# Linear attention and a squared-ReLU feed-forward: keys as weights, split denominators, a new sign step and a new order

## The chip, the cores and the metric

The kernel runs on one core of one Trainium2 chip. The metric is device time in microseconds (us). Three runs of the kernel before gave 237.81, 237.87 and 238.11 us; the median is 237.87 us. One further execution was recorded by the hardware profiler; it took 240.32 us.

## The reference

Four batches, four heads, 1088 positions, head size 32. Each position's q and k become 64 features: eight projections by S1 times eight by S2. For a batch and head, kv is the sum over positions of features times v, and z is the sum of the features; the output at a position is (q features · kv) / (q features · z + 1e-6). The heads side by side make x with 4352 rows and 128 columns, which passes through a feed-forward layer.

```python
def phi(x):
    a = np.einsum('rd,bhsd->bhsr', S1, x)
    b = np.einsum('rd,bhsd->bhsr', S2, x)
    return np.einsum('bhsi,bhsj->bhsij', a, b).reshape(*x.shape[:-1], r * r)
...
kv = np.einsum('bhsf,bhsd->bhfd', k_p, v)
z = np.sum(k_p, axis=2)
num = np.einsum('bhsf,bhfd->bhsd', q_p, kv)
den = np.einsum('bhsf,bhf->bhs', q_p, z)[..., None] + 1e-06
...
r = np.maximum(x @ w_in, 0.0)            # w_in 128 x 2048
return (s * (r * r) + b) @ w_out         # w_out 2048 x 128
```

S1, S2, w_in and w_out come to the chip as 64-bit floats, in two 32-bit words each; q, k and v are 32-bit.

## The kernel before

**Tiles and stages.** The 4352 rows are cut into tile 0 with 256 rows and tiles 1 to 8 with 512. For each batch b, `kvphase(b)` (L239) makes the key features and the matrix st[b] of kv and z: projections on TensorE, transposes on VectorE (L258, L263), the outer product of the two projections (L267), sums over positions on TensorE (L280), a masked copy of z (L294), and products that turn and spread the results (L302, L306). In the first batch keys and values come in three groups of three chunks of 128 positions, in the others in one. In the projections S is the weight and the keys are the moving operand, in quarters of the array. For each tile t, `direct_features` (tiles 0 and 1, L330 to L339) or `stored_features` (the others, with a way through DRAM, L350 to L369) make the q features, and `attend(t)` (L391 to L428) the numerators, denominators, reciprocals and x. Then eight steps `ffn(t, jp)` per tile (L471) do two blocks of 128 of the 2048 columns each: six products into hp, relu, square, and six products into the tile's output sum. In tile 0 the products are plain f32, two and two per step. In tiles 1 to 8 each operand is split into a high part of reduced f32 and a low rest, with three products for one (wih, wil, woh, wol, uh, ul, xh, xl). `finish(t)` (L512) scales the sum and stores it.

**Weights.** `to_float` (L197) makes an f32 of the two words of a 64-bit float in four instructions: the high word scaled (L113, on ScalarE or VectorE), the low word scaled (L119), a join (L190) and the sign put back (L186), the last two on VectorE. `split_weights` follows with the high part (a cast) and the low rest (L448). It is done for S, and for four blocks of 512 columns of w_in and four of w_out, named w0 to w7, even for w_in and odd for w_out.

**What sets the order.** Nothing is scheduled by the compiler. Each piece of work is a generator that issues an instruction group and yields. `ORDER`, a list of names written out, says which generator goes on next, and each engine takes its instructions in that order: y and z are products on constants that do no work for the result, Lx a DMA, s the phase of S, kb the key phase of batch b, qt and nt features and attend of tile t, wx a weight block, and two digits tj the step jp = j of tile t. `ON_DVE` lists the movable instructions that go to VectorE; the others go to ScalarE. All DMAs are issued by SP, in order. At the start they are: a third of the first values (192 KB), S (80 KB), q of tile 0 (128 KB), the first keys (three times 192 KB), q of tile 1 (256 KB), constants (96 KB), the other two thirds of the values, then weight blocks of 512 KB with q of tiles 2 and 3 (256 KB each) between them. The tiles run in the order 0, 1, 2, 3, 4, 5, 8, 6, 7. hp has two buffers of two PSUM banks, the small products share three banks, the output sum has one.

Of the kernel before, what the change touches and what calls it, by code (L numbers as in the profile page):

```python
# [27 lines left out]
NT = len(TILES)  # L28
NCH = 9
SP = NCH * P  # L30
KGROUPS = {0: (3, 3, 3), 1: (9,), 2: (9,), 3: (9,)}
EPS = 1e-6
DIRECT = (0, 1)
DEN_APART = (0,)
FIRST_F32 = (0, 1, 2, 3, 4, 5, 6, 7)
ORDER = """
y y y y y y y y y y y y y y y y y y y y z z z z z z z Lv0 Ls Lq0 Lk0 Lk0 Lk0 s s s Lq1 s Lcst s s s q0 Lv0 q0
Lv0 q0 k0 Lw0 q0 q0 q0 Lw2 k0 Lq2 k0 z k0 Lw1 k0 k0 k0 Lq3 q1 q1 k0 k0 k0 q1 k0 q1 q1 q1 w0 z k0 w0 k0 Lw3 k0
w2 w0 z k0 w2 Lw4 w0 q2 k0 w2 w0 n0 n0 w2 Lw5 q2 Lw6 w1 q3 q2 n0 w1 n0 n0 w2 n0 n0 q3 n0 w3 w2 q3 z 00 w3 w1
n1 00 w1 Lw7 00 w3 01 Lk1 w1 w0 w5 00 n1 01 n1 w5 02 01 n1 w4 w3 w4 q2 01 02 q2 w3 w4 q2 03 02 Lv1 w4 w6 02 q3  # L40
w6 Lq4 w4 04 03 q3 w6 q3 03 w5 05 04 w5 03 04 w6 w5 04 w1 05 n1 06 w7 05 w7 w6 w7 05 06 w7 07 06 n1 w7 06 n1
07 w7 k1 07 n1 w3 n1 07 k1 n1 11 k1 07 07 k1 07 10 11 k1 13 Lq8 10 11 10 12 11 10 11 q4 k1 10 12 10 q4 q2 12
q4 k1 12 13 11 k1 12 13 12 Lv2 w5 13 q3 k1 q8 w6 Lq5 k1 w4 n2 q8 13 15 q8 q4 q4 n2 n2 q4 14 n2 n2 n2 13 14 n2
n2 15 14 n3 15 Lv3 14 16 q8 14 n2 q8 14 q8 15 16 n2 17 16 15 16 22 17 n3 n3 17 n3 20 n3 16 17 15 n3 20 17 16
20 22 17 22 20 20 21 17 n3 22 17 n3 20 n3 21 22 24 21 q4 23 24 21 21 24 Lk3 21 n3 23 22 24 23 24 25 23 q8 27
25 23 23 25 27 27 25 24 27 26 25 25 27 26 Lk2 k2 26 26 32 26 31 32 26 k2 32 k2 k2 32 27 31 k2 30 27 31 27 k2
32 31 k3 31 30 33 30 k2 k3 k3 k2 35 30 33 30 Lq6 30 k3 35 31 35 33 32 k3 33 k2 35 k3 35 k2 q6 k3 q5 33 k3 34
q6 q6 q5 q5 k3 34 n4 k3 34 36 q6 n4 q6 34 n4 q6 37 n4 n4 36 34 33 36 37 36 34 n4 37 n4 n4 35 n4 n4 41 37 36 36
37 41 40 q6 41 37 41 40 41 43 37 40 37 42 43 40 40 43 44 42 43 n8 43 42 45 n8 q5 44 n8 q5 n8 40 n8 q5 44 n8 n8
41 n8 n8 n8 44 Lq7 46 42 42 42 44 45 43 45 46 47 45 q5 46 q7 45 n5 q7 47 44 q7 n5 47 n5 n5 45 n5 46 n5 n5 47  # L50
n5 n6 46 n5 46 n5 q7 q7 47 q7 50 n6 n6 47 n6 50 n6 n6 50 n6 51 n6 50 47 52 51 47 50 51 50 51 52 53 51 52 51 53
q7 52 53 n7 54 52 n7 56 n7 54 53 53 55 54 56 52 n7 54 n7 n7 53 56 n7 n7 54 57 56 55 54 56 81 55 57 57 80 55 55
55 57 81 57 56 81 80 57 81 82 57 81 57 84 80 82 82 80 83 80 82 80 82 83 81 83 84 82 83 84 83 85 84 86 85 84 85
87 86 85 n6 83 n6 n7 85 60 n7 87 84 86 87 86 85 87 86 61 87 60 86 60 61 62 61 60 60 61 64 61 62 87 62 64 65 87
62 87 87 64 87 60 62 64 61 64 65 63 65 66 63 65 65 63 70 66 62 66 63 67 63 63 67 64 67 66 65 66 67 66 70 67 67
70 71 67 70 67 72 71 70 70 71 72 73 72 71 71 74 72 73 72 71 74 73 76 74 73 75 73 74 72 76 74 76 77 75 75 76 73
76 75 74 77 75 75 77 76 77 77 77 77 77
"""
ON_DVE = frozenset("""
a7 a8 k0 q11 q25 q27 q31 q33 q34 q40 q53 q54 q55 q60 q64 q66 q67 q70 q73 q76 q80 q86 r15 r22 r32 r34 r37 r46  # L60
r64 r72 r80 r84 r86 sb t2 t3 u11 u12 u14 u15 u16 u20 u21 u24 u26 u27 u30 u35 u37 u40 u41 u42 u43 u50 u51 u53
u55 u56 u57 u60 u62 u65 u71 u73 u76 u77 u80 u81 u84 u86 w3h w4h w4m w5b w7b w7m x3 x4 x6 x8
# [27 lines left out]
def attn_ffn_kernel(ctx: ExitStack, tc: tile.TileContext, qT, kT, vp, s80, cst, w_in, w_out, outT):  # L90
# [22 lines left out]
    def scaled(key, out, in_, scale):  # L113
        if key in ON_DVE:
            nc.vector.tensor_scalar(out=out, in0=in_, scalar1=scale, scalar2=None, op0=ALU.mult)
        else:
            nc.scalar.activation(out=out, in_=in_, func=AF.Copy, scale=scale)

# [41 lines left out]
    def load_v(b):  # L160
        vt = p2.tile([P, NCH * H * D], F32, name="vt")
        vt = v_in[b] = vt.rearrange("p (c h d) -> p c h d", c=NCH, h=H)
        c = 0
        for n in KGROUPS[b]:
            nc.sync.dma_start(out=vt[:, c:c + n].rearrange("p c h d -> p (c h d)"),
                              in_=block(vp, (b * NCH + c) * H * D, n * H * D))
            c += n
            yield
# [8 lines left out]
    def load_weights(i, k):  # L177
        raw = p4.tile([P, 2 * CW], I32, name=f"raw{k}")
        nc.sync.dma_start(out=raw, in_=block((w_in, w_out)[k], i * CW, CW).bitcast(I32))
        w_raw[i, k] = raw  # L180
        yield
# [3 lines left out]
    def with_sign(out, high, t):  # L185
        nc.vector.scalar_tensor_tensor(out=out, in0=high, scalar=-0x80000000, in1=t,  # L186
                                       op0=ALU.bitwise_and, op1=ALU.bitwise_or)
# [9 lines left out]
    def to_float(key, out, raw, bits):  # L197
        low, high = words(raw)
        scaled(key + "m", out, f32(high), 2.0 ** -112)
# [4 lines left out]
        yield  # L204
        with_sign(out.bitcast(I32), high, out.bitcast(I32))
# [15 lines left out]
    def s_phase():  # L221
# [3 lines left out]
        nc.vector.tensor_copy(out=srep[:, 1].rearrange("p (i x) -> p i x", i=R),  # L225
                              in_=own[:, 1].unsqueeze(1).broadcast_to([P, R, R]))
# [387 lines left out]
```

## Time and profile before

| what | before |
|---|---|
| median of three runs without a profile | 237.87 us |
| profiled execution | 240.32 us |
| span from its first to its last instruction | 237.5 us |
| TensorE products busy | 228.6 us (96%) |
| TensorE weight loads | 176.0 us (74%) |
| VectorE busy | 207.5 us (87%) |
| ScalarE busy | 165.6 us (70%) |
| GpSimd busy | 2.9 us (1%) |
| mean granted clock of TensorE | 0.993 |
| DMA | 22.09 MB, mean 93 GB/s |

Busy times are shares of one profiled execution. TensorE's is the time in which at least one product is under way; products overlap, so a busy TensorE need not be at its peak. A row of the timeline gives the start of an instruction, its duration, the engine, the line, what it writes and reads, and in brackets how long the engine had been idle and what ended that. The chain of waits follows the work that ended last back to the start; each piece is a start, a duration and what ran. A granted clock of 1.00 is 2.4 GHz, one of 0.50 is 1.2 GHz.

### The profile page before, as it was taken

Reading aid. Unit: us, or ns where it says so; the run is one execution under the profiler, and the core shown is the slowest. Engines: PE = TensorE matmul, PEld = TensorE weight load, DVE = VectorE, ACT = ScalarE, POOL = GpSimd, SP = SyncE. Lnnn points to the kernel's source line nnn. Section 1 sums busy time; section 2 is a strip of 40 time slices with the busy share of each in tenths; the row PEclk is TensorE's granted clock in tenths of the full one; section 3 lists DMA queues with packets and bytes.
Section 4 is the critical chain, followed back from the end, with each engine's and each line's share of the span. In section 5 each row is a group of like instructions: output and inputs, shape, how many; then the busy total and the mean of one; then the engine's idle time right before and its main releaser. Section 6 shows DMA issues by size and latency. Waiting matters only on the chain.

```text
span 237.5 us, 4567 instructions
## 1 busy us (share of the span) xinstructions
PE 228.6 (96%) x1864; PEld 176.0 (74%) x1867; DVE 207.5 (87%) x275; ACT 165.6 (70%) x193; POOL 2.9 (1%) x13
## 2 busy tenths in 40 slices
PE   8688999999999999999999999999999999999993
PEld 3556877877887777778878678787878877888782
DVE  1879999999999989989999898999989998577972
ACT  2389978918899548717476677765697797668881
POOL 0000100000000000000000000000000000000000
PEclk9979999999999999999999999999999999999999
DMA  6999974549561002015115344000100001001001
GB/s 168 325 417 366 210 171 151 162 118 188 151 202 68 0 3 91 0 47 135 46 44 150 75 121 122 3 0 1 42 4 0 0 1 44 3 0 44 0 0 44
DMA packets 8948, 22.09 MB, mean 93 GB/s; under 512 B 992, under 2 KB 3424, under 8 KB 8928
## 3 DMA queue, kind: packets, MB, share of 16 engines
q1 hardware_dynamic: 8928, 21.81, 31.5%
q8 instruction: 14, 0.23, 0.4%
q14 instruction: 6, 0.05, 0.1%
HBM read 18.66 MB, written 3.15 MB: 92 GB/s over the span
## 4 chain that ended last, share of the span: by engine, by line
PE 82%; DVE 6%; DMA 4%; ACT 3%; issue 2%; SPq 1%; DVEq 0%; ACTq 0%
PE ops L469 35%; PE hp L469 35%; DMA qt<-qT 4%; PE psa L391 4%; PE psa L280 2%; DVE ul L463 2%; PE psa L350 2%; PE psa L253 1%; PE psa L306 1%; DVE u L133 1%; DVE ph L267 1%; ACT u L129 1%; ACT ot L523 1%; DVE pq L339 1%; DVE uh L111 1%
## 5 line engine op out<-in xcount | busy, mean ns | idle before, releaser
L463 DVE TENSOR_TENSOR ul<-u,uh 128x1024 fp32r<-128x1024 f32 x64 | 77.9, 1222 | 6.6 <-ACT uh L111 3.8
L129 ACT ACTIVATE u<-hp 128x1024 f32<-128x1024 f32 (+1 forms) x61 | 59.2, 970 | 34.2 <-DVE ul L463 18.8
L135 ACT ACTIVATE u<-u 128x1024 f32<-128x1024 f32 (+1 forms) x53 | 52.7, 996 | 5.8 <-DVE u L127 4.4
L469 PE MATMUL hp<-xh,wil 128*128 128x512 f32 x128 | 51.6, 403 | 0.0
L469 PE MATMUL ops<-uh,wol 128*128 128x512 f32 x128 | 50.3, 393 | 0.1
L469 PE MATMUL hp<-xh,wih 128*128 128x512 f32 x128 | 50.0, 390 | 0.0
L469 PE MATMUL hp<-xl,wih 128*128 128x512 f32 x128 | 49.9, 390 | 0.0
L469 PE MATMUL ops<-uh,woh 128*128 128x512 f32 x128 | 49.9, 390 | 0.0
L469 PE MATMUL ops<-ul,woh 128*128 128x512 f32 x128 | 39.8, 392 | 0.0
L111 ACT CAST uh<-u 128x1024 fp32r<-128x1024 f32 x30 | 31.4, 1050 | 8.2 <-DVE u L133 5.5
L469 PEld LDWEIGHTS hp<-xh,wil 128*128 128x128 f32 x128 | 24.0, 188 | 10.1 <-ACT u L129 2.9
L469 PEld LDWEIGHTS ops<-uh,wol 128*128 128x128 f32 x128 | 24.0, 188 | 6.1 <-ACT ot L523 0.5
L469 PEld LDWEIGHTS ops<-ul,woh 128*128 128x128 f32 x128 | 23.6, 188 | 6.0 <-DVE ul L463 1.2
L111 DVE CAST uh<-u 128x1024 fp32r<-128x1024 f32 x34 | 23.4, 690 | 5.2 <-ACT u L135 4.3
L469 PEld LDWEIGHTS hp<-xl,wih 128*128 128x128 f32 x128 | 24.0, 188 | 5.2
L469 PEld LDWEIGHTS ops<-uh,woh 128*128 128x128 f32 x128 | 24.0, 188 | 5.0
L469 PEld LDWEIGHTS hp<-xh,wih 128*128 128x128 f32 x128 | 24.0, 188 | 4.4
L133 DVE TENSOR_TENSOR u<-u 128x1024 f32<-128x1024 f32 x19 | 23.2, 1221 | 2.4 <-ACT u L129 2.3
L127 DVE TENSOR_SCALAR u<-hp 128x1024 f32<-128x1024 f32 x11 | 13.5, 1223 | 1.7 <-PE hp L469 0.9
L523 ACT ACTIVATE ot<-ops,bias,cst_sb 128x512 f32<-128x512 f32 (+1 forms) x10 | 7.0, 709 | 6.4 <-PE ops L469 6.4
L267 DVE TENSOR_TENSOR ph<-kab 128x768 f32<-128x768 f32 (+2 forms) x9 | 10.8, 1222 | 0.2
L391 PE MATMUL psa<-pq,st 64*32 64x256 f32 (+3 forms) x320 | 10.0, 350 | 0.0
(72 smaller groups left out, 172.9 us busy)
## 6 DMA issues: line engine op xcount, KB each, us to landing
pq<-qd SPq DMA_DIRECT2D x7, 512.0 KB
br<-qd SPq DMA_DIRECT2D x14, 256.0 KB
qt<-qT SPq DMA_DIRECT2D x8, 256.0 KB
raw<-w_in SPq DMA_DIRECT2D x4, 512.0 KB
raw<-w_out SPq DMA_DIRECT2D x4, 512.0 KB
outT<-ot SPq DMA_DIRECT2D x7, 256.0 KB
kt<-kT SPq DMA_DIRECT2D x3, 576.0 KB
vt<-vp SPq DMA_DIRECT2D x3, 576.0 KB
```

What stands on the lines that cost most here:

```text
L111: (nc.vector.tensor_copy if key in ON_DVE else nc.scalar.copy)(out=out, in_=in_)
L127: nc.vector.tensor_scalar(out=out, in0=in_, scalar1=0.0, scalar2=None, op0=ALU.max)
L129: nc.scalar.activation(out=out, in_=in_, func=AF.Relu)
L133: nc.vector.tensor_tensor(out=out, in0=in_, in1=in_, op=ALU.mult)
L135: nc.scalar.activation(out=out, in_=in_, func=AF.Square)
L267: nc.vector.tensor_tensor(out=ph[:, c0:c0 + m].rearrange("p c h i x -> p (c h) i x"), in0=a.unsqueeze(3).broadcast_to([P, H * m, R, R]), i ...
L280: nc.tensor.matmul(out[32 * q:32 * q + 32], w, x, start=(q not in begun), stop=last, skip_group_check=True)
L350: nc.tensor.matmul(ab[a:a + 32, :M], sq[:, 32 * w:32 * w + 32], qT_t[t][:, r * M:(r + 1) * M], start=True, stop=True, skip_group_check=True)
L391: nc.tensor.matmul(out[32 * h:32 * h + 32, e0:e1], st_t[b][64 * r:64 * r + 64, h // 2, h % 2, y], pq[64 * r:64 * r + 64, h, e0:e1], start= ...
L463: nc.vector.tensor_tensor(out=ul[:, :, :N], in0=u[:, :, :N], in1=f32(uh[:, :, :N]), op=ALU.subtract)
L469: nc.tensor.matmul(out, w, x, start=(first and k == 0), stop=(last and k == len(terms) - 1))
L523: nc.scalar.activation(out=ot[:, s], in_=o[:, s], func=AF.Identity, scale=s_col, bias=bias)
```

## The change

The change has these parts.

- In the first batch's key phase the keys become the weights and S (64 columns) the moving operand: one product of the full array per chunk of 128 positions. Its result has the positions on the partitions, so the transposes become copies (`first_keys`, k0). The host lays out the first batch's values to match.
- The first batch's sum of keys runs on a path of its own (`first_key_sums`, e0), the values' sums on another (`first_value_sums`, v0), and tile 0's denominators are made from the first alone (`first_denominators`, d0) before its numerators (`first_numerators`, n0).
- `to_float` loses the sign step: the high word goes through a Prelu on ScalarE whose slope for negative numbers is 2^32, and the join's shift leaves a sign from the exponent.
- The first 512 columns of each weight come in two blocks of 256, so there are ten weight blocks, w0 to w9, instead of eight.
- The last tile in the order (7) is finished in two halves, one on ScalarE with a DMA issued by ScalarE, one on VectorE with a DMA issued by SP. Tile 8 is finished in one.
- More constant products at the start, narrower ones (c, 256 columns) between the first phases.
- A new `ORDER` and a new `ON_DVE`; the tiles run 0, 1, 2, 3, 6, 4, 5, 8, 7.

```diff
+VGROUPS = {0: (3, 3, 3), 1: (9,), 2: (9,), 3: (9,)}
+WBLOCKS = (256, 256, 512, 512, 512)
...
+y y y y y y y y y y y y y y y y y y y y y y y y y y y y y y y y y y y y y y y z z z z z z Ls Lk0 Lk0 Lk0 s s
+Lv0 s Lv0 s s s Lv0 Lq0 k0 Lcst Lw0 k0 Lw1 k0 k0 e0 k0 Lw2 c e0 k0 k0 Lq1 v0 Lq2 k0 v0 k0 Lw3 e0 Lw5 c q0 q0
+e0 Lw4 v0 q0 e0 q0 q0 Lw6 w0 v0 q0 w0 Lq4 e0 w0 w1 c c v0 Lk1 w2 v0 w0 w2 w0 Lw7 c d0 q1 w2 w1 d0 w2 q2 w1 d0
+w3 q1 Lw9 d0 q1 d0 w3 Lw8 q1 q2 Lq8 q1 w3 c c n0 w5 q1 n1 w5 Lq5 n0 w4 w5 w4 00 q2 w5 w6 w5 01 w6 w4 00 q4 w6
+00 02 01 w6 q4 n1 Lq3 01 n1 00 q4 n1 n1 w4 Lv1 n1 03 02 w4 Lk3 01 w7 02 w7 04 n1 03 n1 n1 02 w9 03 w9 05 n1 04
+w9 03 04 q2 w7 w9 q2 10 w7 05 q2 w7 q4 05 w9 k1 q4 w3 q4 w8 w3 w8 04 k1 w1 k1 w8 05 10 k1 06 w8 13 10 06 06 07
+w1 10 k1 06 10 k1 w8 07 k3 k1 07 k1 13 k1 k3 07 13 w2 q2 11 13 w6 k1 12 07 11 07 07 13 10 11 k3 11 15 k3 12 n2
+11 12 11 n2 12 k3 15 16 12 12 15 16 n2 16 13 n2 n2 n2 15 14 n2 n2 16 n2 17 15 Lk2 n2 14 q3 Lv3 16 k3 Lv2 q3 14
+q3 17 k2 k3 14 20 k2 k2 17 14 21 q3 k3 q3 k2 20 q3 14 20 k2 15 q4 20 22 20 16 17 k3 17 17 k3 22 q3 q8 17 k2 22
+q8 17 21 q8 n3 k2 22 k2 23 Lq6 21 n3 n3 n3 24 n3 n3 n3 20 n3 n3 n3 21 q5 22 q6 k2 24 21 21 24 q6 23 q6 22 24
+23 q5 24 25 k2 23 n4 25 23 26 25 n4 q6 n4 q6 25 n4 q8 n4 23 n4 q8 26 q8 n4 n4 q6 24 25 26 27 26 26 n4 30 27 n4
+25 30 27 33 27 30 32 27 30 26 30 32 q5 32 27 33 33 32 31 27 32 34 27 33 31 30 33 31 q6 35 34 31 34 n6 31 Lq7
...
+74 73 76 74 73 74 75 76 74 72 74 76 77 75 76 73 76 75 75 77 74 75 77 75 77 76 77 77 77 77 77 77
+a5 a6 b00 k1 k2 q02 q03 q10 q14 q15 q22 q32 q33 q37 q41 q46 q47 q50 q52 q54 q66 q67 q81 r11 r13 r23 r45 r46
+r53 r56 r57 r65 r66 r70 r71 r72 r75 r84 r85 r87 s0 t3 u17 u23 u27 u31 u33 u37 u41 u44 u51 u53 u54 u57 u61 u63
+u67 u70 u72 u73 u74 u75 u77 u80 u81 u85 u86 w0h w5h w6h w7h x1 x2 x3 x6 x8 y0
...
-    def with_sign(out, high, t):
-        nc.vector.scalar_tensor_tensor(out=out, in0=high, scalar=-0x80000000, in1=t,
-                                       op0=ALU.bitwise_and, op1=ALU.bitwise_or)
...
     def to_float(key, out, raw, bits):
         low, high = words(raw)
-        scaled(key + "m", out, f32(high), 2.0 ** -112)
+        nc.scalar.activation(out=out, in_=f32(high), func=AF.Prelu, scale=2.0 ** -112, alpha=2.0 ** 32)
         yield
         scaled_up(key + "b", bits, low.bitcast(U32), 0.875 * 2.0 ** -29, 0.4999)
         yield
         join(out.bitcast(I32), out.bitcast(I32), bits)
-        yield
-        with_sign(out.bitcast(I32), high, out.bitcast(I32))
         yield
...
+        copy("s1", srep[:, 1].rearrange("p (i x) -> p i x", i=R), own[:, 1].unsqueeze(1).broadcast_to([P, R, R]))
+        yield
+        copy("s0", srep[:, 0].rearrange("p (i x) -> p i x", i=R), own[:, 0].unsqueeze(2).broadcast_to([P, R, R]))
...
+    def value_sums(add, out, b, ph, c):
+        for h in range(H):
+            add(h, out, v_in[b][:, c, h], ph[:, c, h].rearrange("p i x -> p (i x)"), c == NCH - 1)
+
+    def masked(out, zz):
+        nc.vector.tensor_tensor(out=out, in0=zz.rearrange("p (h x) -> p h x", h=H).unsqueeze(2).broadcast_to([P, H, R, R]),
+                                in1=mask.unsqueeze(3).broadcast_to([P, H, R, R]), op=ALU.mult)
+
+    def turn_values(out, kvs):
+        nc.tensor.matmul(out, kvs.rearrange("p r f -> p (r f)"), identity, start=True, stop=True, skip_group_check=True)
+
+    def spread(out, zm, first):
+        for h in range(H):
+            for r in range(2):
+                nc.tensor.matmul(out[64 * r:64 * r + 64, h], zm[:, h].rearrange("p i x -> p (i x)"), one32,
+                                 start=(first and h == 0), stop=True, skip_group_check=True)
+
+
+
+    first = {}
+
+    def first_keys():
+        kt = k_in[0]
+        kab = first["kab"] = p1.tile([P, 2, NCH, 32], F32, name="kab0")
+        ph = first["ph"] = p1.tile([P, NCH, H, R, R], F32, name="ph")
+        c0 = 0
+        for n in KGROUPS[0]:
+            ps = ps_a.tile([P, 512], F32, name="psa")[:, :64 * n]
+            for c in range(n):
+                a = (c0 + c) * P
+                nc.tensor.matmul(ps[:, 64 * c:64 * c + 64], kt[:, a:a + P], sk[:, :64],
+                                 start=(c == 0), stop=(c == n - 1), skip_group_check=True)
+            yield
+            copy(f"y{c0}", kab[:, :, c0:c0 + n], ps.rearrange("p (c w x) -> p w c x", w=2, x=32))
+            yield
+            outer(ph[:, c0:c0 + n], kab[:, 0, c0:c0 + n], kab[:, 1, c0:c0 + n], n)
+            yield
+            c0 += n
+
+    def first_key_sums():
+        zt = ps_a.tile([P, 512], F32, name="psa")
+        add = sums()
+        c0 = 0
+        for n in KGROUPS[0]:
+            for c in range(c0, c0 + n):
+                add(c % 4, zt[:, :32], first["kab"][:, 0, c], first["kab"][:, 1, c], c >= NCH - 4)
+            c0 += n
+            yield
+        zm = p2.tile([P, H, R, R], F32, name="zm")
+        masked(zm, zt[:, :32])
+        yield
+        parts = zt[:, P:2 * P].rearrange("p (h d) -> p h d", h=H)
+        spread(parts, zm, True)
+        yield
+        st = st_t[0] = const.tile([P, 2, 2, 2, 32], F32, name="st0")
+        copy("t0z", st[:, :, :, 1], parts.rearrange("p (j g) d -> p j g d", j=2))
+        yield
+
+    def first_value_sums():
+        kvp = ps_a.tile([P, 512], F32, name="psa")
+        add = sums()
+        c0 = 0
+        for n in KGROUPS[0]:
+            for c in range(c0, c0 + n):
+                value_sums(add, kvp[:, :64], 0, first["ph"], c)
+            c0 += n
+            yield
+        kvs = p2.tile([P, 2, 64], F32, name="kvs")
+        copy("k0", kvs, kvp[:, :64].unsqueeze(1).broadcast_to([P, 2, 64]))
+        yield
+        turned = ps_a.tile([P, 512], F32, name="psa")
+        turn_values(turned[:, :P], kvs)
+        yield
+        copy("t0v", st_t[0][:, :, :, 0], turned[:, :P].rearrange("p (j g d) -> p j g d", j=2, g=2))
+        yield
...
+    def first_denominators():
+        M = TILES[0] // 2
+        den = ps_h.tile([P, 2, 512], F32, name="hp")
+        parts_of(0, [den[:, r, :M] for r in range(2)], 1, qfeat[0], True)
+        yield
+        dt = p1.tile([P, NMAX], F32, name="dt")
+        nc.vector.transpose(out=dt[:, :2 * M].rearrange("p (r m) -> p r m", r=2), in_=den[:, :, :M])
+        yield
+        yield from inverse(dt[:, :2 * M], M // 32, first)
+
+    def first_numerators():
+        M = TILES[0] // 2
+        num = ps_h.tile([P, 2, 512], F32, name="hp")
+        parts_of(0, [num[:, r, :M] for r in range(2)], 0, qfeat[0], True)
+        yield
+        x = p2.tile([P, NMAX], F32, name="x")[:, :2 * M]
+        nc.vector.tensor_tensor(out=x.rearrange("p (r m) -> p r m", r=2), in0=num[:, :, :M],
+                                in1=first["rr"][:, :2 * M].rearrange("p (r m) -> p r m", r=2), op=ALU.mult)
+        x_first.append(x)
+        yield
...
+        if t == LAST:
+
+            M = N // 2
+            nc.scalar.activation(out=ot[:, :M], in_=o[:, :M], func=AF.Identity, scale=s_col, bias=bias)
+            yield
+            nc.vector.tensor_scalar(out=ot[:, M:N], in0=o[:, M:N], scalar1=s_col, scalar2=bias,
+                                    op0=ALU.mult, op1=ALU.add)
+            yield
+            nc.scalar.dma_start(out=block(outT, n0, M), in_=ot[:, :M])
+            yield
+            nc.sync.dma_start(out=block(outT, n0 + M, M), in_=ot[:, M:N])
+            yield
+            return
...
+    def keep_warm(n):
...
+        parts = (4, NCH, 32) if b else (1, NCH, P)
+        vp[:, b] = vpad[b].reshape(*parts, H, D).transpose(0, 2, 1, 3, 4).reshape(P, NCH, H, D)
```

Every other call of `copy`, `relu`, `squared` and `split_u` stays; where it runs follows from the new `ON_DVE`. The second, third and fourth batch keep the quarter-array projections and the transposes.

## Rows read from the trace of the kernel before

**Rows 1.** Stretches: start:end, length, busy us by engine, clock, DMA share, GB/s

```profile
10.00:20.00 10.00, 6.92 (x133) 4.41 (x142) 8.52 (x19) 7.25 (x15) 0.00 (x0) 0.83 1.01 390
20.00:30.00 10.00, 10.00 (x74) 8.11 (x59) 9.62 (x21) 9.81 (x18) 1.45 (x4) 1.00 1.02 269
```

**Rows 2.** Chain of waits in order of time: start us, us, what

```profile
18.76 1.13 PE hp L469 x4
...
32.48 0.87 PE ops L469 x4
33.35 1.11 PE psa L253 x16
...
233.62 0.78 ACT ot L523
```

**Rows 3.** Timeline to 13 us, instructions that waited for a DMA or follow one

```profile
3.47 0.27 ACT L117 ACTIVATE sk<-s_raw 128x80 f32<-128x80 f32 x1 [1.46 <-DMA s_raw<-s]
...
8.16 1.15 PE L330 MATMUL hp<-qt,srep 32*64 32x256 f32 x32 [0.24 <-DMA qt<-qT]
...
11.63 0.69 ACT L117 ACTIVATE w<-raw 128x512 f32<-128x512 f32 x1 [1.25 <-DMA raw<-w_in]
...
12.91 0.68 ACT L117 ACTIVATE w<-raw 128x512 f32<-128x512 f32 x1
```

**Rows 4.** Chain of waits, other pieces of TensorE

```profile
15.01 1.01 PE psa L350 x8
...
48.03 0.57 PE psa L350 x8
...
49.83 2.96 PE hp L469 x12
52.79 1.36 PE ops L469 x6
...
54.15 1.02 PE psa L391 x32
...
92.38 0.97 PE psa L253 x16
```

**Rows 5.** Groups of instructions by shape: count, busy us, mean ns, idle before

```profile
L186 DVE SCALAR_TENSOR_TENSOR w<-raw,w 128x512 int32<-128x512 int32 x8 | 5.4, 691 | 0.2
...
L267 DVE TENSOR_TENSOR ph<-kab 128x768 f32<-128x768 f32 x3 | 2.9, 958 | 0.1
...
L523 ACT ACTIVATE ot<-ops,bias,cst_sb 128x256 f32<-128x256 f32 x3 | 1.6, 555 | 0.0
...
L117 ACT ACT_TABLE_LOAD x1 | 1.3, 1283 | 0.7 <-PEq L604 0.7
...
L339 DVE TENSOR_TENSOR pq<-hp,br 128x512 f32<-128x512 f32 x2 | 1.3, 682 | 0.0
```

**Rows 6.** Timeline of ScalarE, consecutive instructions in two places

```profile
17.50 0.61 ACT L111 CAST wih<-w 128x512 fp32r<-128x512 f32 x1
18.01 0.37 ACT L111 COPY abq<-psa 128x256 f32<-128x256 f32 x1
18.27 0.68 ACT L117 ACTIVATE w<-raw 128x512 f32<-128x512 f32 x1
18.84 0.68 ACT L123 ACTIVATE raw<-raw 128x512 int32<-128x512 uint32 x1
...
27.37 0.60 ACT L129 ACTIVATE u<-hp 128x512 f32<-128x512 f32 x1
28.00 0.63 ACT L135 ACTIVATE u<-u 128x512 f32<-128x512 f32 x1
28.54 0.60 ACT L111 CAST woh<-w 128x512 fp32r<-128x512 f32 x1
```

**Rows 7.** Stretches of 1 us, TensorE: busy us, clock, DMA share, GB/s

```profile
11.00:12.00 1.00, 0.14 (x9) 1.00 1.01 377
...
14.00:15.00 1.00, 1.00 (x21) 0.50 1.05 424
```

## Prediction before the run

> **What bounds the kernel now.** I read the table of stretches first. From 20 us on TensorE is busy all of every 10 us at full clock, while the stretch from 10 to 20 us has 6.92 us of it at a mean clock of 0.83 [rows 1]. So two things can shorten the span: TensorE's steady work starting earlier, or less work and fewer waits after it. The chain of waits, read next in order of time, puts the boundary at 18.76 us: VectorE's x of tile 0 ends, the first product of tile 0 starts, and from there the pieces are TensorE's, nearly end to end, until the last output copy at 233.62 us [rows 2]. In the middle of the run the chain also passes through ScalarE and VectorE, but TensorE is full beside them, so that is no loss. Third, the timeline before 20 us shows what the start waits for: the first activation on S data begins at 3.47 us, q of tile 1 is taken at 8.16 us, the first weight block at 11.63 us, all three released by a DMA [rows 3]. From 11.63 us on ScalarE works almost without a pause, 9.81 of the 10 us from 20 to 30, and VectorE 9.62 [rows 1]. So the start is a race of DMA landing, ScalarE and VectorE against a TensorE that could begin.
>
> The profiled execution took 240.32 us with a span of 237.5 us; the median without a profile is 237.87 us. The sum is made inside the span and its difference carried over to the median.
>
> **The start, step by step.** The DMAs are issued by one queue in order, so I count bytes ahead of each landing. Before: S is the second DMA (272 KB with it), q of tile 1 the seventh (1,232 KB), the first weight block the eleventh (2,224 KB), the next weight block ends 2,736 KB. Rows 3 give landings at 3.47, about 8.1, 11.6 and at latest 12.9 us. New order: S 80 KB, keys to 656, values to 1,232, q0 1,360, constants 1,456, then weight halves w0, w1, w2 to 1,712, 1,968 and 2,224, q1 2,480, q2 2,736, w3 2,992. By interpolation on those points: S about 3.0 (one issue earlier), the last values 8.1, q0 8.6, w0 9.8, w1 10.7, w2 11.6, q1 12.3, q2 12.9, w3 13.6 us. A later weight block (w5, w4, w6, 512 KB each) follows every 1.3 us.
>
> S is ready near 3.9 us instead of 4.3: Prelu and its copy follow each other on ScalarE, then one VectorE join, without the sign step. Keys as weights: nine products of 64 columns replace 24 and the three transposes become copies; the trace has no such product, so between the 0.22 us of a full-array f32 product (0.87 us for four [rows 2]) and twice that at half clock, 0.65 to 1.3 us for a group of three; I take 0.65, and it hides behind the values, which land at 8.1 us anyway. The keys' sum, spread and denominators on their own path run on TensorE and VectorE while ScalarE waits for weights. None of this is the last wait; if the values came earlier, the three outer products of 0.96 us each would be [rows 5], ending near 8 us too.
>
> The last wait is ScalarE's queue. In the new order it holds, once w2 has landed at 11.6 us: Prelu, low word and cast of w2, low word of w1, both of w3, the copy of the values' weights, q2's copy, and the two 512-column copies of q1. I price an instruction by the distance to the next start, not by its mean, since neighbours overlap: 0.57 for a 512-column conversion, 0.51 for a cast or copy, 0.26 for a 256-column copy, 0.63 and 0.54 for a relu and its square [rows 6]. A conversion of 256 columns, not in the trace, lies between 0.26 and 0.57; I take 0.29, near the copy of the same width. Ten instructions: 5 x 0.29 + 3 x 0.26 + 2 x 0.51 = 3.25, to 14.85 us. VectorE's second product of q1, 0.68 [rows 5], ends at 15.6. TensorE then does tile 1's numerators and denominators, 1.02 [rows 4], and the first product of tile 0 starts at 16.7 us instead of 18.76; x of tile 0, one VectorE product, lies beside it.
>
> ScalarE meanwhile converts w5, w4 and w6: 6 x 0.57 = 3.4, to 18.3, level with the first relu (product ready at 17.6). From there to the end of w8's low word its queue has relu and square of six pairs (6.7), six more conversions (3.4), two wide casts (1.0) and two narrow ones (0.5): 11.6, to 29.9; the join, 0.69 like the sign step [rows 5], makes w_in of the last block ready at 30.6 us. TensorE over the same piece: 12 steps of tile 0 at 0.87 [rows 2], q4 0.57, one step of tile 1 at 1.36, k1's projection 0.97 and two changes between f32 and reduced f32 at 0.24 (12 products cost 2.96 after such a change and 2 x 1.36 without [rows 4]): 13.8, to 30.5 us. Both meet at 30.6 us, at the first product of step 06.
>
> What remains there is compared with before. At 33.35 us the old kernel [rows 2] has left tile 0's last output step, tiles 1 to 8, all k1 to k3, seven attends and five q projections. The new one at 30.6 us has four steps of tile 0 instead of one (+2.6), but has done one step of tile 1 (-1.36) and k1's projection (-0.97): 0.27 us more. The gain at the start is 33.35 - 30.6 - 0.27 = **2.5 us**.
>
> **The rest.** Sign steps: eight of 0.69 us, 5.4 us of VectorE [rows 5], all in the region where VectorE is full. They are partly what allows the earlier start; by themselves they would be worth nothing without it. Moving the remaining scalings to ScalarE gives ScalarE about 9 us more and VectorE as much less over the run by a count of the instructions; ScalarE was busy 166 of 237.5 us, so in the steady part TensorE covers it. Blocks of 256 columns give two more DMAs and eight more conversions, counted above. SP's queue now waits for a free raw buffer at w9 (w1's join, near 13.5 us) and for q1's tile at q8; behind them stand q5 and q2's store, whose data are due tens of us later, so nothing; if the cover were gone, w8 would be late by what the wait is over, at most 1 us. The mid-run order: the f32 groups stand between reduced f32 groups in 12 places instead of 11, which costs 0.25 us more. The end: the last copy of 512 columns takes 0.78 us, of 256 columns 0.56 [rows 2, 5], with VectorE's half beside it: 0.2 us less; the two DMAs issue from two queues beside each other, and the trace has no issue from ScalarE, so between 0.3 us lost and 0.3 won; I take nothing.
>
> Sum: 2.5 + 0.2 - 0.25 = 2.45 us. Span 237.5 to 235.05, profile 240.3 to 237.9, median 237.87 to **235.4 us**.
>
> **The Trainium skill against it.** Before shows one table load of 1,283 ns for Copy, Relu, Square and Identity together [rows 5]. The Trainium skill, "ScalarE: Activation LUTs", section "Table sets: the hidden batching unit", says that functions come in sets of which one is active, that cheap ones are in every set, and that each change of set costs a load and a drain, about 2.7 us. It doesn't say where Prelu and Square stand together. By the trace's load alone it is the third rival below; by the page's figure that rival would be twice as dear.
>
> **Rivals.**
> *Earlier.* The weight halves land one by one, and the first 656 KB are S and keys alone. If w2 is there at 10.6 us, ScalarE's whole queue moves and TensorE starts 00 near 15.7: 3.5 us, 234.4 us. For it: DMA moved 390 GB/s between 10 and 20 us [rows 1]. Against: the landings before, which kept to 283 KB per us.
> *Half clock.* Before, TensorE idles from 11 to 12 us (0.14 busy) and is granted 0.50 at 14 us [rows 7], the 1.2 GHz level; a q projection then took 1.01 us instead of 0.57 [rows 4]. The new order has filler products, but the same thin stretch. If the half clock falls on 13 to 17 us: q2 and the second half of q1 end 0.8 us later, the attend takes twice its 1.02 us: 00 starts 1.9 us later, the next products also lose 0.3; 0.3 us remain, 237.6 us.
> *Slower: ScalarE's queue.* Every wait from 11.6 to 30.6 us stands behind that queue, and Prelu is in no row. If Prelu and Square share no table, loads stand at the first square, at w7's Prelu and the square after it, the same at w9, and at w8: six by 29.9 us, 7.7 us at 1.28 each. Step 06 is then at 38.3: 243.1 us. It decides from two loads on, or from 2.5 us that Prelu costs over Copy in that stretch. For it: Prelu alternates with Square there. Against: the four other functions share one load.
> If the change didn't do what it says, that is, if start and keys were not on the path, the time would stay at 237.9.
>
> **How the numbers follow.** Forecast 0.52 (234.5 to 236.6), earlier 0.13, half clock 0.20, ScalarE's queue 0.15. About 0.2%, 0.5 us, is what a measurement tells from no change. Faster: the forecast, the earlier case and 0.04 of the half clock: 0.69. Same: 0.12 of the half clock and 0.03 of a queue that just eats the gain: 0.15. Slower: 0.16. The range reaches from the earlier case with 0.8 us more, 233.6, to 238.2, a half clock that costs 0.6 us more than reckoned; outside are most of the queue's case and the tails.
>
> **What would show it.** First product of tile 0 at 16 to 17.5 us, ScalarE without a pause from about 11.6 to 30 us, first product of step 06 near 30.6 us, one table load, VectorE busy near 198 us and ScalarE near 175, a TensorE that is full from 00 on, and a last copy of 0.56 us. Wrong, if TensorE shows holes between 17 and 35 us, if 00 starts after 18 us, or if ScalarE holds more than one table load.

## The result, and the profile after

The kernel after takes **235.69 us** at the median (235.21 to 235.91, four runs), the kernel before 237.91 us beside it (237.81 to 238.11, four runs): a ratio of 0.990, 95% interval 0.989 to 0.992. The prediction was 235.4 us. So the number came out; the reasons came out in part only.

| what | after |
|---|---|
| profiled execution | 235.21 us |
| span | 233.3 us |
| TensorE products busy | 227.7 us (98%) |
| TensorE weight loads | 179.1 us (77%) |
| VectorE busy | 201.1 us (86%) |
| ScalarE busy | 171.9 us (74%) |
| mean granted clock of TensorE | 1.000 |

The stretches of after that answer to [rows 1] (columns as there): TensorE has 9.61 instead of 6.92 us between 10 and 20 us, and its clock stays at 1.00.

```profile
10.00:20.00 10.00, 9.61 (x183) 5.33 (x167) 9.25 (x22) 9.40 (x24) 0.06 (x1) 1.00 0.98 375
20.00:30.00 10.00, 10.00 (x60) 7.84 (x57) 9.76 (x22) 9.94 (x20) 1.17 (x4) 1.00 1.03 364
```

The chain of waits of after, against [rows 2]: q of tile 0 lands at 9.44, the chain then runs through ScalarE's queue, tile 0's first products are the piece from 17.63 us and step 06 is in the piece that starts at 31.68 us. (A piece of the chain starts where the one before it ends; in TensorE's own timeline, the single line after it, tile 0's first product starts at 17.56 us. First products further on are read there.) TensorE ends at 229.53 us, and two output copies follow one another.

```profile
4.01 5.43 DMA qt<-qT
...
10.38 0.37 ACT br L113
...
15.22 0.57 ACT br L113
...
15.82 0.70 DVE pq L391
...
16.56 1.07 PE psa L432 x24
17.63 1.92 PE hp L540 x8
...
31.68 3.11 PE hp L540 x14
...
229.56 0.57 ACT ot L593
...
230.15 0.54 DVE ot L595
```

```profile
17.56 1.99 PE L540 MATMUL hp<-x,w 128*128 128x256 f32 x8
```

ScalarE's timeline of after, the part that answers to [rows 6]: from 10.38 to 30 us one pause, of 0.16 us. A conversion of 256 columns takes 0.44 us, and by the distance to the next start, the prediction's measure, 0.34 (two of them from 11.61 to 12.29).

```profile
10.64 0.44 ACT L193 ACTIVATE w<-raw 128x256 f32<-128x256 f32 x1
...
11.61 0.79 ACT L193 ACTIVATE w<-raw 128x256 f32<-128x256 f32 x2
12.29 0.26 ACT L113 COPY st<-psa 128x128 f32<-128x128 f32 x1
12.44 0.79 ACT L119 ACTIVATE raw<-raw 128x256 int32<-128x256 uint32 x2
13.38 0.41 ACT L113 CAST wih<-w 128x256 fp32r<-128x256 f32 x1 [0.16 <-DVE w L184]
```

Groups of after by shape, against [rows 5]: the conversion with Prelu takes 692 ns where the one with Copy took 677, and there is still one table load.

```profile
L193 ACT ACTIVATE w<-raw 128x512 f32<-128x512 f32 x6 | 4.2, 692 | 0.0
...
L193 ACT ACT_TABLE_LOAD x1 | 1.3, 1283 | 0.7 <-PEq L683 0.7
```

**Where the time went.** I cut both spans at the output copies of tile 1 and of the last tile (TensorE has the start behind it at the first of them). ScalarE's timeline of before gives 66.38 and 233.62 us, that of after 68.72 and 229.56 us; the spans end at 237.45 and 233.34 us:

| part of the span | before | after | difference |
|---|---|---|---|
| to the copy of tile 1 | 66.38 | 68.72 | +2.34 |
| from it to the last copy | 167.24 | 160.84 | -6.40 |
| from the last copy to the end | 3.83 | 3.79 | -0.05 |

After does more of TensorE's work ahead of the first cut, so the counts have to be compared. These are TensorE's groups in the long stretch, of before and then of after (the six groups of reduced f32 products, three of which stand for the others here).

```profile
L469 PE MATMUL ops<-uh,wol 128*128 128x512 f32 x112 | 44.0, 393 | 0.1
...
L469 PE MATMUL hp<-xh,wil 128*128 128x512 f32 x108 | 43.3, 400 | 0.0
...
L253 PE MATMUL psa<-kt,sk 128*32 128x288 f32 x32 | 2.3, 409 | 0.0
L350 PE MATMUL psa<-qt,sq 128*32 128x256 f32 x24 | 1.7, 386 | 0.1
```

```profile
L540 PE MATMUL ops<-uh,wol 128*128 128x512 f32 x112 | 44.0, 393 | 0.0
...
L540 PE MATMUL hp<-xh,wil 128*128 128x512 f32 x106 | 41.7, 394 | 0.0
...
L402 PE MATMUL psa<-qt,sq 128*32 128x256 f32 x32 | 2.3, 388 | 0.0
```

A reduced f32 product follows the one before it by 0.2267 us (12 of them take 2.72 in the chain). Before: 3 x 112 + 3 x 108 = 660 of them, 149.6 us; two key phases at 0.97, 1.31, 0.22 and 0.59; three q projections at 0.57; five attends, three at 1.02 and two at 1.23: 163.0 us in all, and 4.2 us over. After: 654, 148.3 us; one key phase without its projection, 2.2; four q projections, 2.2; six attends, 6.5: 159.2 us, and 1.6 us over. So 3.8 us of the 6.4 is work that after has done earlier, and **2.6 us is time that TensorE lost between products before and does not lose after**. By the same reckoning the start of this pair gained 3.8 - 2.34 = 1.5 us and the end 0.05 us: together 4.1 us, the difference of the spans.

### The profile page after: what moved, and what is told of

It is laid out like the page before. It is cut to its first block, busy times and chain, and to the rows that moved or that the text cites. A ratio compares the mean times of both kernels' runs of the same rounds, so it can differ in the third digit from the quotient of the medians.

```text
span 233.3 us, 4610 instructions
## 1 busy us (share of the span) xinstructions
PE 227.7 (98%) x1876; PEld 179.1 (77%) x1877; DVE 201.1 (86%) x262; ACT 171.9 (74%) x207; POOL 2.8 (1%) x13
## 4 chain that ended last, share of the span: by engine, by line
PE 92%; DMA 2%; ACT 2%; SPq 1%; DVE 1%; issue 0%
PE hp L540 41%; PE ops L540 41%; PE psa L432 4%; DMA qt<-qT 2%; PE psa L239 2%; PE psa L402 1%; PE psa L330 1%; PE psa L258 1%; ACT br L113 1%; SPq L161 1%; SPq L152 1%; PE psa L253 0%; ACT w L193 0%; ACT raw L119 0%; PE hp L382 0%
## 5 line engine op out<-in xcount | busy, mean ns | idle before, releaser
L125 ACT ACTIVATE u<-hp 128x1024 f32<-128x1024 f32 (+1 forms) x55 | 52.9, 962 | 25.6 <-DVE ul L534 13.5
L131 ACT ACTIVATE u<-u 128x1024 f32<-128x1024 f32 (+1 forms) x54 | 54.5, 1013 | 7.8 <-DVE u L123 6.7
L540 PE MATMUL hp<-xh,wil 128*128 128x512 f32 x128 | 51.0, 399 | 0.0
L113 ACT CAST uh<-u 128x1024 fp32r<-128x1024 f32 x39 | 40.7, 1050 | 4.1 <-DVE u L129 3.0
L123 DVE TENSOR_SCALAR u<-hp 128x1024 f32<-128x1024 f32 x17 | 20.8, 1222 | 3.4 <-PE hp L540 2.5
L113 DVE CAST uh<-u 128x1024 fp32r<-128x1024 f32 x25 | 17.3, 691 | 4.9 <-ACT u L131 4.1
L129 DVE TENSOR_TENSOR u<-u 128x1024 f32<-128x1024 f32 (+1 forms) x18 | 20.9, 1162 | 0.1
L603 ACT ACTIVATE ot<-ops,bias,cst_sb 128x512 f32<-128x512 f32 (+1 forms) x8 | 6.0, 750 | 8.7 <-PE ops L540 8.7
```

The costliest lines, as they stand in the source:

```text
L113: (nc.vector.tensor_copy if key in ON_DVE else nc.scalar.copy)(out=out, in_=in_)
L123: nc.vector.tensor_scalar(out=out, in0=in_, scalar1=0.0, scalar2=None, op0=ALU.max)
L125: nc.scalar.activation(out=out, in_=in_, func=AF.Relu)
L129: nc.vector.tensor_tensor(out=out, in0=in_, in1=in_, op=ALU.mult)
L131: nc.scalar.activation(out=out, in_=in_, func=AF.Square)
L540: nc.tensor.matmul(out, w, x, start=(first and k == 0), stop=(last and k == len(terms) - 1))
```

## The experiments

The ratios are against runs of before on the same chip. The runs below were made on three chips, and before itself took 238.3 to 238.7 us on them, so times of different experiments compare to a few tenths of a us only.

**c_before** and **c_after**: both kernels again, unchanged, each beside the experiments of its chip.

> The kernel before, unchanged, for a second trace. Theory A (the gain is the earlier start): first product of tile 0 near 18.8 us again, half clock between 13 and 17 us again, span near 237. Rival B (the traced execution of before was an unusual one, 240.32 us against a median of 237.9): no half clock, first product near 17.5 to 18 us, span 235 to 236. Rival C (short stalls of TensorE in the steady part make up the difference): some 7 groups of reduced-f32 products that take about 0.25 us more than 1.36 us per six without an f32 group before them, in this trace too.

> The changed kernel, unchanged, for a second trace and the spread of its start. Theory C (the gain is in the steady part, whose time is fixed by order and engine assignment, and the start only scatters): from the output copy of tile 1 to the last product 160.8 to 160.9 us as in the first trace, the first product of tile 0 anywhere from 17.2 to 18.3 us. Theory A (the gain is the start): first product within 0.3 us of 17.56 us.

Before: a span of 237.4 us in the profiled run, where the median of 17 spans on that chip is 236.4. Its clock was at 1.00 throughout, and yet tile 0's first product started at 19.00 us. The chain of waits of this run tells why:

```profile
5.91 8.42 DMA raw<-w_in
...
15.65 0.70 DVE w L190
...
16.38 0.69 DVE w L186
17.07 0.37 DVE dt L400
...
19.00 1.13 PE hp L469 x4
```

A weight block landed at 14.34 us, and tile 0's denominators stood on VectorE behind its join and its sign step. So the late start doesn't need the half clock of [rows 7]. What the half clock cost in the first trace isn't told apart by this: there a q projection of 1.01 us stands in the chain where 0.57 is usual [rows 4]. After: 235.44 us (234.6 to 237.71), ratio 0.988 (0.983 to 0.992), tile 0's first product at 17.70, the stretch between the two copies 160.89 us.

**h_mid** and **h_start**: before's code and start with after's order and assignment from tile 0's end on, and after's with those of before from the middle of tile 1 on. In h_mid the second half of tile 8's output is left out, in h_start the last steps of tile 7's.

```diff
 h_mid, ORDER of before: all names up to the fourth 07 stay
-k1 n1 11 k1 07 07 k1 07 10 11 k1 13 Lq8 10 11 10 12 11 10 11 q4 k1 10 12
+Lq8 Lq5 q4 q4 q4 Lk3 n1 10 q4 q4 q4 k1 k1 10 k1 13 10 10 k1 10 k1 k3 k1
...
```

> The kernel before, with its own code and order up to the last output step of tile 0 (35.5 us), and from there the order and the engine assignment of the changed kernel. Theory A: no gain, 237.5 to 238.1. Rival C: 236.0 to 236.8, since the short stalls of the steady part go.

> The changed kernel with its own order up to the output step of jp = 5 of tile 1 (about 56 us), and from there the order and the engine assignment of the kernel before. Theory A: the whole gain of the start is kept, 235.4 to 235.9. Rival C (the steady part carries the gain): 236.8 to 237.6, with short stalls after 56 us as in the kernel before.

250.5 us (1.050, 1.047 to 1.053) and 248.0 us (1.040, 1.037 to 1.043): at the seams TensorE had only 6.6 to 9.1 us of every 10 between 30 and 80 us in h_mid, and similar holes to 110 us in h_start, so the totals say nothing on either theory. But h_mid's run behind the seam is clean, and it can be read alone: the copies of tile 1 and of the last tile stand at 81.27 and 242.14 us, 160.87 us apart. With before's code and before's start the long stretch takes what it takes in after. The 2.6 us come from the order and the assignment, not from the new start or its code.

**m_assign_a** and **m_assign_b**: is it the order or the assignment? The movable instructions of the middle of the run on the engines of the other kernel.

```diff
 m_assign_a, ON_DVE of after; m_assign_b is the same step on before
-a5 a6 b00 k1 k2 q02 q03 q10 q14 q15 q22 q32 q33 q37 q41 q46 q47 q50 q52 q54 q66 q67 q81 r11 r13 r23 r45 r46
+a7 a8 b00 k1 q02 q03 q11 q25 q27 q31 q33 q34 q40 q53 q54 q55 q60 q64 q66 q67 q70 q73 q76 q80 q86 r15 r22 r32
...
```

> The changed kernel with its own order, but for tiles 1 to 8 the choice of engine (VectorE or ScalarE) of the kernel before: 72 instead of 66 entries on VectorE, of these 34 instead of 25 casts, 19 instead of 16 squares and 11 instead of 17 relus. If the assignment took the short stalls away, they come back: from tile 1's copy to the last product 162.5 to 165 us instead of 160.85. If the order did it, 160.8 to 161.3.

> The kernel before with the engines that after gives to the movable instructions of the middle of the run (relu, square, low parts, casts of tiles 1 to 8, the later key phases); order and start as before. Theory A, order and assignment are fitted to each other: the steady part, 167.2 us in before and 160.9 in after, grows by 5 us or more, as it grew by 14.5 us when after's order ran with before's assignment. Theory B, the assignment by itself brings the gain: the steady part falls by 1 us or more.

253.84 us and 272.31 us, one run each. The long stretch took 175.3 us with after's order (160.8 with its own assignment), and about 197 with before's order (167.2 with its own). Each order ran well with its own assignment only; which of the two brings the 2.6 us can't be said apart.

**e_sign**: after with the sign step.

```diff
-        nc.scalar.activation(out=out, in_=f32(high), func=AF.Prelu, scale=2.0 ** -112, alpha=2.0 ** 32)
+        nc.scalar.activation(out=out, in_=f32(high), func=AF.Copy, scale=2.0 ** -112)
...
         join(out.bitcast(I32), out.bitcast(I32), bits)
+        with_sign(out.bitcast(I32), high, out.bitcast(I32))
```

> The changed kernel with the sign step back: ten more VectorE instructions before 31 us, 6 x 0.6 + 4 x 0.4 = 5.2 us, and a copy instead of the Prelu on ScalarE. Theory A, in which VectorE is full from 10 us on and ScalarE's queue and TensorE bind: the join of the last weight block comes 2 to 4 us later, 237 to 238.5. Rival (VectorE has room at the start, the sign step was hidden): 235.7 to 236.2.

241.44 us (238.88 to 242.52), 1.010 (1.006 to 1.014) of before, 3.0 us above it, and more than either theory said. The profiled run is the fastest of the twelve; its stretches show where: TensorE has holes from 20 to 40 us, VectorE is full, ScalarE is not.

```profile
20.00:30.00 10.00, 8.97 (x46) 6.97 (x38) 9.72 (x20) 7.18 (x14) 1.51 (x4) 1.00 1.00 339
30.00:40.00 10.00, 8.10 (x97) 5.83 (x99) 9.86 (x15) 7.31 (x13) 0.61 (x2) 1.00 0.64 152
```

Its long stretch takes 160.89 us like that of after. So the new start can't do without the freed VectorE time.

**b_nosign**: the reverse, before without the sign step.

```diff
-        scaled(key + "m", out, f32(high), 2.0 ** -112)
+        nc.scalar.activation(out=out, in_=f32(high), func=AF.Prelu, scale=2.0 ** -112, alpha=2.0 ** 32)
...
-        with_sign(out.bitcast(I32), high, out.bitcast(I32))
```

> The kernel before with only the sign step taken out: Prelu on ScalarE in to_float, order, assignment and everything else as before. Theory A, the sign steps bind the old start: in the second trace of before, tile 0's denominators stood on VectorE behind the join and the sign step of a weight block whose DMA landed at 14.34 us. One sign step of 0.69 us less ahead of them lets the first product of tile 0 start near 18.3 instead of 19.0 us, the later ones free VectorE up to 33 us, and the time falls by 0.7 to 2 us. Theory B, the prediction's sentence that the sign steps would be worth nothing by themselves because the old order does not use the free time: no change, within 0.5 us of before, and the first product of tile 0 at 18.5 us or later. The steady part from the output copy of tile 1 on stays at 167 us in both.

238.9 us (238.53 to 242.31), 1.002 (0.999 to 1.005): no change. Theory B held in its main point, though the first product of tile 0 started earlier than it expected, at 17.73 us. (The edit also moves the two conversions that before had on VectorE to ScalarE.) VectorE's load between 20 and 30 us fell from 9.62 [rows 1] to 5.23 us, ScalarE had 9.87 and TensorE even lost 0.23:

```profile
20.00:30.00 10.00, 9.77 (x44) 7.88 (x44) 5.23 (x14) 9.87 (x19) 1.58 (x5) 1.00 0.95 248
```

In before's order ScalarE is as full there as VectorE, so this room on VectorE is worth nothing there.

**e_keys** and **e_noc**: one part of the new start undone at a time.

```diff
 e_keys, first_keys (and the values' layout to match)
-                nc.tensor.matmul(ps[:, 64 * c:64 * c + 64], kt[:, a:a + P], sk[:, :64],
...
+                    nc.tensor.matmul(views[w][32 * q:32 * q + 32], sk[:, 32 * w:32 * w + 32], kt[:, a:a + w32],
...
-            copy(f"y{c0}", kab[:, :, c0:c0 + n], ps.rearrange("p (c w x) -> p w c x", w=2, x=32))
+            nc.vector.transpose(out=kab[:, :, c0:c0 + n],
+                                in_=ps[:, :2 * w32].rearrange("p (w t) -> p w t", w=2))
 e_noc, ORDER: the seven c
-c
```

> The kernel after with the first batch's keys as the moving operand again: quarter-array products and three VectorE transposes (0.374 us each in the trace of before) in place of nine full-array products and three copies (two on ScalarE, one on VectorE). Order and all else as after. Theory A, the prediction's: the phase hides behind the values and q of tile 0, so the time stays within 0.4 us of after and the first product of tile 0 stays at 17.3 to 17.9 us. Theory B, VectorE binds from the keys on: two more VectorE instructions of 0.37 us and the longer products push the outer products and all that stands behind them by 0.7 to 1.5 us, and the time rises by as much.

> The kernel after without the narrow constant products between the first phases (the c of the order, which do no work for the result). Theory A: the clock does not bind the start, the time stays within 0.4 us of after; TensorE is idle for some tenths more between 10 and 17 us. Theory B, the prediction's half-clock rival: without them the granted clock falls to 0.50 somewhere between 11 and 17 us, the first product of tile 0 comes 1 to 2 us later and the time rises by 1 to 2 us.

235.19 us (234.4 to 238.72) and 235.24 us (234.37 to 236.73), 0.986 and 0.985 of before (0.981 to 0.990 and 0.989). After itself has 0.988 and was not run on this chip, so a part that is worth more than about 1 us would show; neither does. Their profiled runs, 237.47 and 236.73 us, were among the longest of their sets, and show the half clock that the prediction had feared, with tile 0's first product at 19.32 and 18.63 us. Stretches of e_noc, TensorE alone (us, busy, clock, DMA share, GB/s): a block of w_out landed only at 13.99 us, TensorE was busy for 0.85 of the 2 us from 14 to 16, and was granted 0.50 (1.2 GHz) after that; tile 1's 32 products of the attend then took 2.45 us instead of 1.02 [rows 4].

```profile
14.00:15.00 1.00, 0.55 (x12) 1.00 1.00 397
15.00:16.00 1.00, 0.30 (x20) 0.96 1.04 420
16.00:17.00 1.00, 1.00 (x30) 0.50 1.04 414
```

```profile
8.40 5.59 DMA raw<-w_out
...
16.25 2.45 PE psa L433 x32
```

That run's span is 234.8 us, the other five have 232.4 to 233.5 and clocks from 0.997 to 1.000: late landing and half clock together cost some 1.8 us in this run. e_keys, which has the fillers, shows both in its profiled run too.

**e_q0**: after with q of tile 0 and the constants loaded ahead of the values, to move ScalarE's queue.

```diff
-Lv0 s Lv0 s s s Lv0 Lq0 k0 Lcst Lw0 k0 Lw1 k0 k0 e0 k0 Lw2 c e0 k0 k0 Lq1 v0 Lq2 k0 v0 k0 Lw3 e0 Lw5 c q0 q0
+Lq0 s Lcst s s s Lv0 Lv0 Lv0 k0 Lw0 k0 Lw1 k0 k0 e0 k0 Lw2 c e0 k0 k0 Lq1 q0 q0 v0 Lq2 k0 v0 k0 Lw3 e0 Lw5 c
...
```

> The changed kernel with q of tile 0 and the constants issued before the values, and the features of tile 0 ahead of the values' sums. Theory: ScalarE's queue starts at q0's landing (9.4 us); q0 now lands near 7 us, ScalarE's first feature copy starts near 9 us instead of 10.4, then the weight blocks bind: first product of tile 0 0.4 to 0.9 us earlier, 235.0 us. Rival: the weight blocks' landing binds anyway, no change.

235.22 us (234.89 to 235.72), 0.986 (0.983 to 0.989), the first product of tile 0 at 17.35 us. q's features are through earlier, and then the next wait stands at the same place: q of tile 1 lands at 12.11 us in this run's chain, its projections run to 14.97, and its second copy and product follow.

```profile
6.39 5.71 DMA qt<-qT
...
12.24 1.09 PE hp L383 x16
...
14.99 0.59 ACT br L114
...
17.42 1.92 PE hp L541 x8
```

**e_tail**: after with a tile of its own for VectorE's half of the last output.

```diff
+            ot1 = p2.tile([P, NMAX], F32, name="ot1")
-            nc.vector.tensor_scalar(out=ot[:, M:N], in0=o[:, M:N], scalar1=s_col, scalar2=bias,
+            nc.vector.tensor_scalar(out=ot1[:, M:N], in0=o[:, M:N], scalar1=s_col, scalar2=bias,
...
```

> The changed kernel with VectorE's half of the last output in a tile of its own. In the trace of the changed kernel this half waited for ScalarE's (230.15 us after 229.56). If the wait comes from the two halves sharing a tile, both start together near the end of the last product, and the end comes 0.5 us earlier (0.2%). Rival: the wait is on the shared PSUM bank or on the bias, and nothing changes.

235.17 us (234.9 to 237.7), 0.988 (0.984 to 0.993): no change against c_after. VectorE's half still waits for ScalarE's, in e_tail's timeline as in that of after:

```profile
229.93 0.54 DVE L596 TENSOR_SCALAR ot<-ops,cst_sb,bias 128x256 f32<-128x256 f32 x1 [1.98 <-ACT ot L594]
```

So the written tile isn't the cause. What the two halves still share is what they read: the output sum, one PSUM bank, and the bias and scale columns. The Trainium skill, "PSUM — Partial Sum Buffer", section "PSUM bank collisions raise a hardware error", says that the compiler's scheduler puts a dependency between any two engines that touch one bank in the same partitions, reads too; the wait shown here agrees, but neither a sum in two banks nor a bias of its own was tried.

No variant is shown to beat after: c_after, e_q0 and e_tail on one chip, e_keys and e_noc on another lie within 0.3 us of each other.

## Why the prediction was right, and where it wasn't

**The start, forecast 2.5 us.** The picture was right: a nearly contiguous ScalarE, 9.40 and 9.94 us, one table load, step 06 in a piece that starts at 31.68 instead of 30.6 us. The size was not. q of tile 0 landed at 9.44 instead of 8.6 us, and ScalarE's queue had been waiting for it, not for w2. So w2's conversion began at 11.95 instead of 11.6 us. The 256-column conversion, priced at 0.29 us from start to start, takes 0.34, 0.25 us more for the five, and a join on VectorE held the queue up for 0.16 us. In the queue to 29.9 us the six pairs of relu and square are 7.0 us by the prediction's own prices, not 6.7. And the projections of q of tile 1, which end the chain in e_q0, stood in no term. In place of 16.7 the first product came at 17.56 us, and 1.5 of the 2.5 us were left in the two profiles.

But those two are not a fair pair. The long stretch hardly varies (167.24, 166.98 and 167.03 us in the three traces with before's order, 160.84 to 160.90 in eight with that of after), so what differs between the traces of a kernel is the start. The profiled start of before was slow: a span of 237.5 us, against a median of 236.1 on the chip that ran c_after; the profiled run of after was the fastest of its four. With the long stretch and the end taken off, the usual start on that chip is 236.1 - 167.0 - 3.8 = 65.3 us before and, with c_after's median span of 233.65, 233.65 - 160.9 - 3.8 = 68.95 us after, 3.65 us later with 3.8 us more done: next to no gain. On the chip of e_keys and e_noc the same working, with median spans of 236.8, 233.45 and 233.0 us, leaves a gain of 1.0 and 1.5 us. So the start gained between nothing and 1.5 us; the runs don't resolve it, but 2.5 it was not. The profiled execution of before, 240.32 us against a median of 237.87, warned of this from the outset; the prediction carried its whole start over to the median.

**The steady part, forecast 0.25 us lost.** This is the step that failed: "TensorE is full beside them, so that is no loss" and the eye on one table of busy shares. In the long stretch TensorE's busy time is 166.87 of 167.24 us before and 160.80 of 160.84 us after, full both times, yet 4.2 and 1.6 us are lost. A product runs 0.39 us and the next starts after 0.227 us, so a pause of up to 0.16 us does not show as idle at all. The timeline of TensorE in before shows one, 0.30 us between the first two starts where 0.23 is usual, and the chain of waits shows it as a group of 12 that takes more than 2.72 us:

```profile
163.78 0.39 PE L469 MATMUL hp<-xl,wih 128*128 128x512 f32 x1
164.08 0.49 PE L469 MATMUL hp<-xh,wil 128*128 128x512 f32 x1
164.41 0.39 PE L469 MATMUL hp<-xh,wih 128*128 128x512 f32 x1
```

```profile
71.78 2.96 PE ops L469 x12
...
162.81 2.90 PE hp L469 x12
...
172.54 1.65 PE hp L469 x6
...
196.11 3.02 PE ops L469 x12
...
225.04 1.63 PE hp L469 x6
```

Seven groups in each kernel are late by 0.22 to 0.27 us because a group of f32 stands ahead of them: 1.7 us, all that after loses. Eight more groups in before are late by 0.11 to 0.30 us with no f32 ahead, 1.7 us together, and on two stretches its chain leaves TensorE, from 124 to 135 us for a q tile and from 180 to 196 us through ScalarE and VectorE. What these eight groups wait for is not in the row of the products but in that of the weight loads. A load usually follows the one before it after 0.04 us; at each of the eight places it stands idle for 0.22 to 0.54 us and names who ended the wait. Four waited for a relu on ScalarE (L129), which reads the hp buffer that the next products write, three for a low rest from VectorE (L463), and one for the copy of the output sum (L523). One of each kind:

```profile
72.62 0.30 PEld L469 LDWEIGHTS ops<-ul,woh 128*128 128x128 f32 x2 [0.36 <-DVE ul L463]
...
164.08 0.19 PEld L469 LDWEIGHTS hp<-xh,wil 128*128 128x128 f32 x1 [0.34 <-ACT u L129]
...
196.11 0.19 PEld L469 LDWEIGHTS ops<-uh,wol 128*128 128x128 f32 x1 [0.54 <-ACT ot L523]
```

All three traces with before's order have these eight waits, of nearly the same length; after and h_mid have none of them, and m_assign_a has more of the kind, up to 2.2 us long. Over the whole run the loads ahead of a new hp group show it, in before and then in after:

```profile
L469 PEld LDWEIGHTS hp<-xh,wil 128*128 128x128 f32 x128 | 24.0, 188 | 10.1 <-ACT u L129 2.9 <-ACT uh L111 0.9 <-issue 0.7
```

```profile
L540 PEld LDWEIGHTS hp<-xh,wil 128*128 128x128 f32 x128 | 24.0, 188 | 6.9 <-issue 1.0 <-DVE u L129 0.5 <-ACT uh L113 0.4
```

The prediction saw the chain leave TensorE and waved it off. The change between f32 and reduced f32, which it priced at 0.25 us more, costs the same in both here.

The Trainium skill, "Perfetto Trace Analysis", section "Identifying the Most-Contended Engine", warns that the busy share of matmuls is no good measure of TensorE, since they are pipelined, and points to the share of weight loads. The traces agree: weight loads take 130.85 of 167.24 us before and 128.88 of 160.84 after, 78 and 80%, where the busy share says 100 and 100.

**The end, forecast 0.2 us won.** 0.05 us: the halves run one behind the other, 0.56 and 0.54 us, which takes longer than one copy of 0.78, and the shorter last transfer makes up for it. "Beside it" was the wrong word.

**The rivals.** Earlier: no, 17.56 us. The queue with a second table: no, one load, and Prelu costs 15 ns more than Copy. The half clock exists in single runs, together with a late landing, at about the price reckoned, but the medians don't carry it. VectorE was forecast near 198 and has 201.1 us, ScalarE near 175 and has 171.9.

So the 2.2 us measured are, by the runs, about 2.4 to 2.6 us of waits that a new order and assignment took out of the long stretch and 0.05 us at the end, which leaves nothing for the start in that measurement. The forecast overrated the start and missed the long stretch; the two errors have opposite signs and are about as large as the effect. That the total came out near 235.4 us was luck. What stays open is whether the order or the assignment made relus, low rests and copies come in time.

## What to carry to other kernels

Count a full engine's instructions and multiply by the distance of their starts; what the stretch takes beyond that is loss, whatever the busy share says. For TensorE, look for the cause in the row of the weight loads. Before a start is priced from one profile, compare that run with the median of the runs: a profile 1% above it shows a start that is not the usual one. An engine freed in a stretch where another is just as full gives nothing, but an order that relies on the room falls apart without it.

## What the runs showed of the hardware that was not expected

From tile 1's output on, eight traces with after's order and assignment repeat to 0.06 us (160.84 to 160.90), on several chips, while the spans of one kernel differ by 2 to 3 us (232.8 to 235.9 in c_after). In the traces the difference stands ahead of tile 1's output: its copy starts at 68.72 us in after and at 69.67 in c_after. An ACTIVATE that converts 256 columns of every second 32-bit word takes 0.34 us from start to start where one of 512 takes 0.57, and a copy of 256 columns that reads PSUM 0.26. A start as late as that of before with the half clock (18.76 us) came without it in c_before (19.00), and an earlier one with it in b_nosign (17.73); in e_noc, where it fell on tile 1's attend, that attend took 1.4 us more. Pauses of TensorE under 0.16 us between products leave no idle time in the row of the products and do leave it in the row of the weight loads.
